# Windowed attention feeding a gated network: the values of a head step in one load of 120 rows of 4 KB, in place of three loads

## The chip, the cores and the metric

The kernel runs on one core of one Trainium2 chip. The metric is the time of one execution on the device in microseconds (us); lower is better.

## The reference: what is computed

Two parts follow each other. The first is attention with B = 4 batches, H = 8 heads, S = 768 positions and D = 64 columns a head, all float32. Each position sees the keys closer than 16 positions and, of every block of 32 positions, one summary: the maximum of the block's keys and the mean of its values (24 summaries a batch).

```python
k_sum = k.reshape(B, H, nb, block, D).max(axis=3)
v_sum = v.reshape(B, H, nb, block, D).mean(axis=3)
scores_l = where(|i - j| < window, scale * q @ k^T, -1e9)
scores_s = scale * q @ k_sum^T + log(block)
a = softmax over concat([scores_l, scores_s])      # with 1e-9 added to the sum
x = a @ concat([v, v_sum])                         # 3072 tokens x 512 columns
h = (x @ w1) * (x @ w2) @ w3                       # 1024 columns
return h @ w_out                                   # 3072 x 512
```

## The kernel before

**Staging.** The kernel works on 6 units of 512 tokens, each with 4 pairs of heads: 24 attention steps `s = (u, p)`. A step covers 4 blocks of 128 tokens. Each block of 128 is worked as two halves `g` of 64 rows; a half needs 96 local keys or values and the 24 summaries, 120 (`KR`) in all. `CUT` is 96 and `NB` is 24.

A step goes through these stages:

- `load_scores` brings `q` and `k`, and `load_values` (line 276) the values `v`, all by DMAs issued on SyncE (SP). `v` has 120 rows (the contraction of the output product), then half, block, and 128 columns: 4 KB a row, in two buffers. For `g = 0` the rows 0 to 95 are local and 96 to 119 summaries; for `g = 1` the rows 0 to 31 are local, 32 to 55 summaries (the gap), 56 to 119 local.
- `load_sums` (line 285) writes the summaries of the values into `v`: for batch 0 two copies on GpSimd (POOL, line 294), for later batches DMAs from SBUF to SBUF on SP (line 291). `gather` (line 306, POOL) writes those of the keys into `k`.
- `scores` (line 319, TensorE, which the profile calls PE), `reduce` (line 333, VectorE, called DVE: mask and minimum), `expose` (line 347, ScalarE, called ACT: the exponentials), `invert` (line 352 on POOL, line 353 on DVE), `normalize_alone` (line 362 on ACT, 364 on DVE) in steps 0 to 7 or `normalize` (line 356, POOL) later.
- `transposes` (line 373, PE, tiles `tp`), `evacuate` (line 378 on ACT for `pt[0]`; line 380 on ACT or 382 on DVE for `pt[1]`, as `SECOND` says), `outputs` (line 393, PE, tile `po`, reads `pt` and `v`), `keep_x` (line 404 on ACT, line 109 on DVE: `x` as a high part and a rounding rest).

**The network.** Every weight arrives as 64-bit words in pieces of 512 KB (`wraw`, line 147) and is rebuilt in `convert`: line 167 on ACT, lines 175 and 178 on DVE, then the high part by a cast on ACT (line 188) and the low part on DVE (line 109, in `low`). `w3 @ w_out` is folded once into `wp` (`fold_weights`; the product leaves PSUM by line 211 on ACT and line 109 on DVE). After the folds, `gate` does the two products of a unit with `w1` and `w2`, and `project` the product with `wp`. All these products are at line 113, three passes each.

**The order.** In the first phase (steps 0 to 7, some 130 us) the order of SP and PE is written by hand: the tables `LOADS` and `WORK` and the tuple `FIRST` say at which count of weight pieces something is loaded, prepared or begun. The order of ACT, DVE and POOL there is chosen when the program is built, by a scheduler that works from its own estimates. In the later loop (steps 8 to 23, by twos) PE, ACT and DVE are in the order of the code. On SP, a DMA takes one of 8 completion semaphores in turn (`DMAHW0` to `DMAHW7` below), and an instruction that waits keeps everything behind it on its engine waiting.

The values of steps 0 to 7 are called for by `LOADS` (15, 21, 25, 28) and `WORK` (29, 37, 42, 46), the summaries by `WORK` alone:

```python
19: [lambda: fetch_sums(0)],
21: [..., lambda: fetch_sums(1)],
22: [..., lambda: fetch_sums(2)],
28: [lambda: fetch_sums(3)],
29: [lambda: fetch_values(4), lambda: fetch_sums(4)],
37: [..., lambda: fetch_values(5), ..., lambda: fetch_sums(5)],
```

Of the kernel before, what the change touches and what calls it, by code (L numbers as in the profile page):

```python
# [19 lines left out]
P = 128  # L20
# [4 lines left out]
CUT = 96  # L25
BIG = -8.0e9
TOKENS = 512
# [43 lines left out]
def attention_moe(ctx, tc, qG, kW, kT, vP, vW, vB, mask, w1, w2, w3T, wo, out):  # L71
    nc = tc.nc
    B, NPAIR, _, S = kT.shape
    NB = S // BLOCK
# [6 lines left out]
    D = P // 2  # L81
    KR = CUT + NB
# [193 lines left out]
    def load_values(u, p):  # L276


        v = sb.tile([KR, 2, NBLK, P], F32, name="v", bufs=2)
        nc.sync.dma_start(v[:CUT, 0], vW[u, p, 0])  # L280
        nc.sync.dma_start(v[: CUT - 64, 1], vW[u, p, 1, : CUT - 64])
        nc.sync.dma_start(v[KR - 64 :, 1], vW[u, p, 1, CUT - 64 :])
        return v

    def load_sums(u, p, v):
# [229 lines left out]
    def fetch_values(s):  # L515
        if s < NS:
            values[s] = load_values(*place(s))
# [257 lines left out]
```

## Time and profile before

| what | value |
|---|---|
| median of 3 runs | 540.87 us (540.83 to 541.28) |
| the profiled execution | 540.83 us, of which the profile's span is 539.0 us |
| mean granted clock of TensorE | 0.989 |
| busy share of the span: PE, weight loads of PE, DVE, ACT, POOL | 96%, 78%, 44%, 44%, 10% |
| DMA of the whole execution | 67.21 MB, mean 125 GB/s |

A row of the profile that gives an instruction has its start in us from the span's beginning, its duration in us, the engine, the line, the operation and the tiles `out<-in`; in brackets stand the idle time of the engine just before it and what ended it. A row `A <- B: x, n, y` counts the waits of A for B: sum in us, how many, and the longest. A row that starts with `a:b` is a window, with the busy time of each engine in it, the granted clock of TensorE (1.00 is full), the DMA share and GB/s.

### The profile page before, as it was taken

The page shows a single profiled execution, that of the slowest core. Times are in us where ns is not written, and L with a number is a line of the kernel's source. Part 1 is how long each engine was busy: PE and PEld are TensorE (multiplying, and loading weights), DVE is VectorE, ACT ScalarE, POOL GpSimd, SP SyncE. Part 2 cuts the span into 40 slices and gives each one's busy share as a digit, 9 for nine tenths or more (in the row PEclk, how much of TensorE's full clock was granted, in tenths as well). Part 3 has the DMA queues.
Part 4 walks back from the last instruction along what each step waited for, and adds up shares of the span by engine and source line. Part 5 has one row for each costly group of instructions (what it writes and reads, how often), then busy time and mean ns, then how long its engine had stood idle before and what let it go on. Part 6 is the DMA issues. An engine that isn't in the chain of part 4 may idle for free.

```text
span 539.0 us, 9912 instructions
## 1 busy us (share of the span) xinstructions
PE 517.9 (96%) x3852; PEld 421.8 (78%) x3852; DVE 237.5 (44%) x686; ACT 238.9 (44%) x688; POOL 56.3 (10%) x103
## 2 busy tenths in 40 slices
PE   2897999999999999999999999999999999999997
PEld 1655777888788888888888888888888888888885
DVE  5868889999503226724244033252042351122210
ACT  5547898887345225226235144253162261222210
POOL 1001221111001101103003002011021020000000
PEclk9988899999999999999999999999999999999999
DMA  8999689956524005544032141050160020000001
GB/s 309 403 348 350 189 270 369 280 183 197 167 96 154 0 1 169 162 128 135 0 111 60 40 152 58 0 157 33 40 190 1 1 75 39 21 21 0 1 19 58
DMA packets 30574, 67.21 MB, mean 125 GB/s; under 512 B 4032, under 2 KB 7616, under 8 KB 30528
## 3 DMA queue, kind: packets, MB, share of 16 engines
q1 hardware_dynamic: 27072, 60.30, 35.2%
q10 hardware_dynamic: 3456, 6.29, 3.1%
q8 instruction: 30, 0.49, 0.4%
q14 instruction: 16, 0.13, 0.1%
HBM read 58.51 MB, written 6.29 MB: 120 GB/s over the span
## 4 chain that ended last, share of the span: by engine, by line
PE 91%; DVE 3%; ACT 3%; DMA 1%; issue 1%; POOL 0%; SPq 0%; POOLq 0%; ACTq 0%
PE mm L113 79%; PE po L393 5%; PE sc L319 4%; PE tp L373 2%; DVE w L109 1%; DMA wraw<-in_w3T_dram 1%; DVE wf L178 1%; ACT w L188 1%; PE means L260 1%; ACT sm L347 1%; DVE wf L175 1%; ACT wf L167 0%; ACT wp L211 0%; DVE wp L109 0%; POOL k L306 0%
## 5 line engine op out<-in xcount | busy, mean ns | idle before, releaser
L113 PE MATMUL mm<-x,w 128*128 128x512 f32 x1152 | 264.9, 390 | 0.0
L113 PEld LDWEIGHTS mm<-x,w 128*128 128x128 f32 x1152 | 215.4, 188 | 45.6 <-issue 0.5
L113 PE MATMUL mm<-wp,h 128*128 128x512 f32 x576 | 133.9, 391 | 0.0
L113 PEld LDWEIGHTS mm<-wp,h 128*128 128x128 f32 x576 | 107.5, 188 | 22.7 <-issue 0.2
L347 ACT ACTIVATE sm<-sm,mx 128x120 f32<-128x120 f32 x192 | 73.6, 387 | 19.9 <-DVE mx L333 19.9
L438 DVE TENSOR_TENSOR g<-mm,g 128x512 f32<-128x512 f32 x48 | 33.1, 689 | 90.6 <-PE mm L113 88.7
L439 ACT CAST h<-g 128x512 fp32r<-128x512 f32 x48 | 29.6, 618 | 87.7 <-DVE g L438 87.7
L113 PE MATMUL mm<-w,w 128*128 128x512 f32 x192 | 54.1, 435 | 12.6 <-ACT w L188 11.5
L113 PEld LDWEIGHTS mm<-w,w 128*128 128x128 f32 x192 | 38.2, 206 | 25.6 <-ACT w L188 13.3
L457 ACT COPY o<-mm 128x512 f32<-128x512 f32 x24 | 14.1, 585 | 81.3 <-PE mm L113 81.3
L109 DVE TENSOR_TENSOR h<-g,h 128x512 fp32r<-128x512 f32 x48 | 35.7, 743 | 24.2 <-ACT h L439 24.0
L435 ACT COPY g<-mm 128x512 f32<-128x512 f32 x48 | 28.0, 584 | 35.6 <-PE mm L113 35.2
L333 DVE CUSTOM_DVE_ANT_0 sm<-sc,mask_sb 128x120 f32<-128x120 f32 x192 | 41.0, 275 | 5.5 <-PE sc L319 5.5
L382 DVE COPY pt<-tp 120x512 f32<-120x512 f32 x19 | 12.4, 686 | 67.7 <-PE tp L373 67.7
L306 POOL COPY k<-ks 128x96 f32<-128x96 f32 (+1 forms) x32 | 10.1, 327 | 252.3 <-DMA k<-in_kW_dram 210.0
L347 ACT ACTIVATION_READ_ACCUMULATOR sm<-sm,mx 128x1 f32 x192 | 36.5, 190 | 0.0
L109 DVE TENSOR_TENSOR x<-po,x 128x512 fp32r<-128x512 f32 x24 | 16.6, 690 | 42.2 <-ACT x L404 42.2
L356 POOL TENSOR_TENSOR sm<-sm,mx 128x960 f32<-128x960 f32 x16 | 29.1, 1820 | 6.0 <-DVE mx L353 5.0
L167 ACT ACTIVATE wf<-wraw 128x512 f32<-128x512 f32 x40 | 26.1, 669 | 6.2 <-DMA wraw<-in_wo_dram 2.7
L188 ACT CAST w<-wf 128x1024 fp32r<-128x1024 f32 (+1 forms) x25 | 21.9, 875 | 12.8 <-DVE wf L178 12.7
L393 PEld LDWEIGHTS po<-pt,v 120*64 120x64 f32 x768 | 23.8, 138 | 4.7 <-issue 2.9
L109 DVE TENSOR_TENSOR w<-wf,w 128x1024 fp32r<-128x1024 f32 (+1 forms) x25 | 25.4, 1014 | 4.4 <-ACT w L188 4.1
(33 smaller groups left out, 281.1 us busy)
## 6 DMA issues: line engine op xcount, KB each, us to landing
k<-in_kW_dram SPq DMA_DIRECT2D x24, 368.0 KB
wraw<-in_w3T_dram SPq DMA_DIRECT2D x16, 512.0 KB
wraw<-in_w_dram SPq DMA_DIRECT2D x16, 512.0 KB
q<-in_qG_dram SPq DMA_DIRECT2D x24, 256.0 KB
raw<-in_kT_dram SPq DMA_DIRECT2D x16, 384.0 KB
out_dram<-o ACTq DMA_DIRECT2D x24, 256.0 KB
v<-in_vW_dram SPq DMA_DIRECT2D x24, 192.0 KB
raw<-in_vB_dram SPq DMA_DIRECT2D x12, 384.0 KB
```

The source lines that it names most:

```text
L109: eng.tensor_tensor(dst, src, hi.bitcast(F32), ALU.subtract)
L113: nc.tensor.matmul(acc, lhsT=a, rhs=b, start=first and i == 0, stop=last and i == len(terms) - 1)
L167: nc.scalar.activation(f[:, k * PIECE : (k + 1) * PIECE], words[:, :, 1].bitcast(F32), AF.Prelu, scale=2.0**-112, alpha=-(2.0**32),)
L188: nc.scalar.copy(hi, f)
L319: nc.tensor.matmul(sc[h][64 * g : 64 * g + 64, i * KR : (i + 1) * KR], lhsT=q[rows, i * P + 64 * g : i * P + 64 * g + 64], rhs=k[rows, i, ...
L333: nc.vector.tensor_tensor_reduce(out=sm[:, j], in0=sc[h][:, i * KR : (i + 1) * KR], in1=mask_sb[:, 0 if blk == 0 else 2 if blk == BLOCKS - ...
L347: nc.scalar.activation(sm[:, j], sm[:, j], AF.Exp, bias=mx[:, 0, j : j + 1], scale=-1.0, accum_out=mx[:, 1, j : j + 1])
L356: nc.gpsimd.tensor_tensor(sm, sm, mx[:, 2].unsqueeze(2).broadcast_to([P, NI, KR]), ALU.mult)
L393: nc.tensor.matmul(po[cols, at : at + 64], lhsT=v[:, g, i, cols], rhs=pt[g][:, (h * NBLK + i) * 64 : (h * NBLK + i + 1) * 64], start=True, ...
L435: nc.scalar.copy(g, a[:, :U])
L438: nc.vector.tensor_tensor(g, acc[1][:, :U], g, ALU.mult)
L439: nc.scalar.copy(h[:, 0], g)
```

## The change

The host lays the values out as they lie on the chip, with zeros in the rows that belong to summaries, and one DMA of 120 rows of 4 KB loads them all. It writes the rows of the summaries too, so the instructions of `load_sums` are ordered behind it. Nothing else is edited. Lines behind the edit have numbers lower by 2.

```diff
@@ load_values
         v = sb.tile([KR, 2, NBLK, P], F32, name="v", bufs=2)
-        nc.sync.dma_start(v[:CUT, 0], vW[u, p, 0])
-        nc.sync.dma_start(v[: CUT - 64, 1], vW[u, p, 1, : CUT - 64])
-        nc.sync.dma_start(v[KR - 64 :, 1], vW[u, p, 1, CUT - 64 :])
+        nc.sync.dma_start(v, vW[u, p])
         return v
@@ on the host
-    wins = wins.reshape(B * S // TOKENS, TOKENS // P, 2, CUT, H // 2, 2 * D)
-    vW = wins.transpose(0, 4, 2, 3, 1, 5)
+    wins = wins.reshape(B * S // TOKENS, TOKENS // P, 2, CUT, H // 2, 2 * D).transpose(0, 4, 3, 2, 1, 5)
+    vW = np.zeros((*wins.shape[:2], CUT + NB, *wins.shape[3:]), v.dtype)
+    vW[:, :, :CUT, 0] = wins[:, :, :, 0]
+    vW[:, :, : CUT - 64, 1] = wins[:, :, : CUT - 64, 1]
+    vW[:, :, CUT + NB - 64 :, 1] = wins[:, :, CUT - 64 :, 1]
```

The order of PE's instructions stays as it was, and SP has 190 rows where it had 240. In the first phase the scheduler puts ACT, DVE and POOL in another order. The numbers behind names of tiles count instructions and shift with the change: `w_895` before is `w_887` after, and `w_977` is `w_969`.

On ACT, around the output product of step 3 (`w_895` and then `w_977` are weights being rebuilt, `wp_87` the last of the 8 folded tiles, `pt` the transposed softmax of step 3), before:

```order
L188 CAST w_895<-wf 128x1024
L167 ACTIVATE wf<-wraw 128x512 x2
L211 CAST wp_87<-mm 128x512
L188 CAST w_977<-wf 128x1024
L378 COPY pt<-tp 120x512
L167 ACTIVATE wf<-wraw 128x512
```

and after:

```order
L188 CAST w_887<-wf 128x1024
L167 ACTIVATE wf<-wraw 128x512 x2
L188 CAST w_969<-wf 128x1024
L211 CAST wp_87<-mm 128x512
L376 COPY pt<-tp 120x512
L167 ACTIVATE wf<-wraw 128x512 x2
```

The cast of the later weight piece has moved ahead of the folded product; the copy `pt` follows both, as before.

On DVE at the same place, before:

```order
L109 TENSOR_TENSOR w_895<-wf,w_895 128x1024
L175 TENSOR_SCALAR wf<-wf 128x1024
L178 SCALAR_TENSOR_TENSOR wf<-wraw,wf 128x512 x2
L109 TENSOR_TENSOR wp_87<-mm,wp_87 128x512
L382 COPY pt<-tp 120x512
L109 TENSOR_TENSOR w_977<-wf,w_977 128x1024
```

and after:

```order
L109 TENSOR_TENSOR w_887<-wf,w_887 128x1024
L175 TENSOR_SCALAR wf<-wf 128x1024
L178 SCALAR_TENSOR_TENSOR wf<-wraw,wf 128x512 x2
L109 TENSOR_TENSOR w_969<-wf,w_969 128x1024
L109 TENSOR_TENSOR wp_87<-mm,wp_87 128x512
L380 COPY pt<-tp 120x512
```

The low part of the later weight piece has moved from behind the copy `pt` to a place ahead of the folded product's low part.

On SP at step 4, with what each instruction waits for (names with `DMAHW` are landings of earlier DMAs by their semaphores, `_49` only part of the name; each load waits for the one that had its semaphore before), before:

```order
L147 DMA wraw<-in_w_dram 128x1024 [waits DMAHW2_49,Activation_49]
L280 DMA v<-in_vW_dram 96x512 [waits DMAHW3_49]
L281 DMA v<-in_vW_dram 32x512 [waits DMAHW4_49]
L282 DMA v<-in_vW_dram 64x512 [waits DMAHW5_49]
L291 DMA v<-vs 24x2x128 [waits DMAHW6_49,DVE_49]
L291 DMA v<-vs 24x2x128 [waits DMAHW7_49]
L147 DMA wraw<-in_w_dram 128x1024 [waits DMAHW0_49,Activation_49]
```

and after:

```order
L147 DMA wraw<-in_w_dram 128x1024 [waits DMAHW2_49,Activation_49]
L280 DMA v<-in_vW_dram 120x1024 [waits DMAHW3_49]
L289 DMA v<-vs 24x2x128 [waits DMAHW4_49,DMAHW3_49,DVE_49]
L289 DMA v<-vs 24x2x128 [waits DMAHW5_49]
L147 DMA wraw<-in_w_dram 128x1024 [waits DMAHW6_49,Activation_49]
```

Two instructions are gone, and the first summary now waits for the load just ahead of it (`DMAHW3_49`), in addition to what it waited for.

## The prediction

> **What bounds the kernel now.** I read the page first (busy shares, the slices, the chain that ended last), then the waits of TensorE, then the order of time around each of them, and last the windows with the granted clock.
>
> ```profile
> PE 517.9 (96%) x3852; PEld 421.8 (78%) x3852; DVE 237.5 (44%) x686; ACT 238.9 (44%) x688; POOL 56.3 (10%) x103
> PE 91%; DVE 3%; ACT 3%; DMA 1%; issue 1%; POOL 0%; SPq 0%; POOLq 0%; ACTq 0%
> ...
> 60.00:90.00 30.00, 29.09 (x330) 22.81 (x327) 26.24 (x78) 26.84 (x83) 6.77 (x13) 1.00 0.83 263
> 90.00:120.00 30.00, 30.00 (x200) 24.30 (x198) 28.19 (x58) 26.29 (x71) 4.35 (x9) 1.00 0.80 249
> ```
>
> The first row is busy time of each engine, the second the shares of the chain. TensorE (PE) is busy 96% of the span. The last two rows are windows (length; busy PE, PEld, DVE, ACT, POOL; granted clock; DMA share; GB/s): from 90 us on PE never stops, so whatever delay or gain reaches it before 90 us stays to the end, one for one. But from 60 to 120 us ScalarE (ACT) and VectorE (DVE) are 88 to 94% busy too. There the kernel has almost no slack in the order in which these two serve PE.
>
> ```profile
> PE mm L113 <- ACT w L188: 11.5, 3, 9.5
> PE tp L373 <- DVE wp L109: 3.9, 2, 2.4
> PE mm L113 <- DVE w L109: 1.1, 2, 0.5
> PE po L393 <- ACT pt L378: 0.7, 2, 0.5
> PE sc L319 <- POOL k L306: 0.4, 1, 0.4
> ```
>
> These are all waits of PE. The first and third are the start, up to 28 us; the first value load is issued only at 25.9 us (rows below), so they cannot change. No wait names a DMA: the transfers that the change touches are not in PE's way. What is left to gain is 3.9 + 0.5 + 0.4 us, what there is to lose is the slack of ACT and DVE.
>
> **The change, part by part.**
>
> *Three loads become one.* 24 times, two DMA instructions of SP go away.
>
> ```profile
> L280 SPq DMA_DIRECT2D v<-in_vW_dram x24: 319/370/892, 25.9 to 434.1; - x24
> L282 SPq DMA_DIRECT2D v<-in_vW_dram x24: 515/598/1173, 26.9 to 435.1; - x24
> 30.00:60.00 30.00, 26.12 (x182) 18.56 (x180) 23.96 (x62) 20.07 (x55) 3.76 (x8) 0.84 1.00 325
> 14.00:30.00 16.00, 12.98 (x49) 9.15 (x49) 13.29 (x21) 8.63 (x15) 0.00 (x0) 0.98 1.03 402
> ACT wf L167 <- DMA wraw<-in_w_dram: 1.4, 1, 1.4
> 118.93 0.69 ACT L167 ACTIVATE wf<-wraw 128x512 f32<-128x512 f32 x1 [1.45 <-DMA wraw<-in_w_dram]
> ```
>
> SP saves the second and third issue, 0.4 to 0.6 us each, some 1.0 us per step, and it is only a queue: that costs nothing and gains nothing unless a transfer is waited for. The bytes grow from 384 to 480 KB. At the 325 GB/s of the window of 30 to 60 us that is 1.51 us for 1.21, at 402 GB/s (the window in which rows of 4 KB prevail) 1.22: between 0 and +0.3 us of DMA time per load. I take 0.1, since the new rows are of the 4 KB kind. The Trainium skill ("DMA: Bandwidth & Descriptors", "Why a DMA increments its semaphore by 16 and not by 1", on how many engines) has a rule against the change: the engines used are the largest number up to 16 that divides the rows, so 120 rows go over 15 engines where 96, 32 and 64 went over 16. By it 8 rows fall to an engine, as in a load of 128 rows, and the sum stays what it is, since no row of PE waits for these loads. The cover is the lead of the loads: the last two rows are the only wait of ACT for a DMA between 30 and 130 us, 1.4 us at 118.93, and PE does not feel it. So 0, bounds 0 to +0.3 for the few loads before 90 us.
>
> *The gap is written twice, so a summary waits for its load.* The single load covers the gap; the copies of summaries on POOL (line 294) and their DMAs on SP (line 291) must wait for it to land, where before they went ahead of it. On POOL the scale of the softmax sums (line 352) and the copies into `k` (line 306) queue behind; on SP the loads that follow. This also leads to another order on POOL.
>
> ```profile
> 60.20 1.26 POOL L294 COPY v<-vs 24x512 f32<-24x512 f32 x2 [1.99 <-PE po L393]
> 61.53 1.36 POOL L306 COPY k<-ks 128x96 f32<-128x96 f32 x2
> 62.73 1.05 PE L319 MATMUL sc<-k,q 64*64 64x120 f32 x32 [0.40 <-POOL k L306]
> 70.24 1.15 PE L393 MATMUL po<-pt,v 120*64 120x64 f32 x32
> ```
>
> Before, the copy of summaries (1.26 us) stood ahead of the keys' copies and PE lost 0.40 us at 62.73. In the new order the keys go first, so this wait goes: -0.40. What is late next is the output product of step 1 (70.24 us): ACT now does one unpacking and one weight cast (0.57 + 0.94) between the exponentials and the copies of the transposes, which then end about 70.4. The 0.40 us is given back there; the sum of both is 0 (-0.4 to +0.4).
>
> *ACT and DVE are put in another order (the term that decides).* The order of the instructions, listed above for both kernels, shows it: the cast of `w_969` stands ahead of `wp_87` and of the copy `pt` on ACT, and its low part ahead of `wp_87` and `pt` on DVE. Before, it went like this:
>
> ```profile
> 81.75 1.05 ACT L188 CAST w<-wf 128x1024 fp32r<-128x1024 f32 x1
> 82.83 1.23 DVE L109 TENSOR_TENSOR w<-wf,w 128x1024 fp32r<-128x1024 f32 x1
> 84.69 1.29 DVE L178 SCALAR_TENSOR_TENSOR wf<-wraw,wf 128x512 uint32<-128x512 uint32 x2
> 85.74 0.59 ACT L211 CAST wp<-mm 128x512 fp32r<-128x512 f32 x1 [1.80 <-PE mm L113]
> 86.22 1.05 ACT L188 CAST w<-wf 128x1024 fp32r<-128x1024 f32 x1
> ...
> 86.36 0.69 DVE L109 TENSOR_TENSOR wp<-mm,wp 128x512 fp32r<-128x512 f32 x1 [0.37 <-ACT wp L211]
> 86.97 0.68 DVE L382 COPY pt<-tp 120x512 f32<-120x512 f32 x1
> 87.17 0.59 ACT L378 COPY pt<-tp 120x512 f32<-120x512 f32 x1
> 87.81 1.15 PE L393 MATMUL po<-pt,v 120*64 120x64 f32 x32 [0.52 <-ACT pt L378]
> 88.89 3.94 PE L113 MATMUL mm<-x,w 128*128 128x512 f32 x16
> ...
> 65.20:83.90 18.70, 18.70 (x188) 14.68 (x187) 16.54 (x43) 18.70 (x63) 3.43 (x8) 1.00 0.81 239
> ```
>
> I put the new order through with these durations. From the exponentials of step 2 to the cast at 81.75, ACT is without a pause before (last row, a window as above: ACT busy 18.70 of 18.70 us) and, I take it, after; the new order has one unpacking more in that stretch (0.57) and one less ahead of it, of which some 0.3 is won (the rest goes to a wait for PE), so it is 0.25 us late: DVE's unpacking of this weight (84.69 + 1.29) ends at 86.23. Only then can the cast start, since it needs it: 86.25 + 1.05 = 87.30. `wp_87` and the first `pt` follow on ACT (0.48 from start to start, then 0.59): the first `pt` is there at 88.3. On DVE the low part starts at 87.33, `wp_87` 1.13 later (the spacing of such rows), `pt` 0.61 after that, and it takes 0.68: the second `pt` is there at 89.75. Of the output product's 16 matmuls two need the first `pt` alone, and the third the second, so 14/16 of 1.08 us follow on 89.8: the gate products start at 90.75 where they started at 88.89. That is +1.86 us on PE, with bounds +0.9 (DVE 0.25 early and its neighbours closer) to +2.4 (ACT late by a whole unpacking). Nothing hides it: PE has no other work in its fixed order.
>
> *The clock.* A stall of PE has a second price here.
>
> ```profile
> 26.00:29.40 3.40, 1.72 (x6) 1.15 (x7) 2.25 (x4) 1.62 (x2) 0.00 (x0) 0.99 1.03 399
> 29.40:32.70 3.30, 3.30 (x9) 2.52 (x9) 2.61 (x6) 1.28 (x3) 0.57 (x1) 0.50 1.06 357
> 46.40:49.80 3.40, 0.99 (x5) 0.40 (x3) 3.00 (x6) 3.40 (x9) 0.24 (x1) 1.00 1.08 241
> 49.80:53.20 3.40, 1.94 (x36) 1.81 (x39) 3.37 (x6) 1.80 (x4) 0.00 (x0) 0.50 1.02 355
> ...
> 28.41 5.53 PE L113 MATMUL mm<-w,w 128*128 128x512 f32 x16 [0.53 <-DVE w L109]
> 88.89 13.92 PE L113 MATMUL mm<-x,w 128*128 128x512 f32 x60
> ```
>
> The columns are as above; the granted clock is the third from the right. Both times that PE was busy for only 0.99 or 1.72 of 3.40 us, the next 3.4 us were granted half the clock. Sixteen products took 5.53 us across such a stretch, where 60 take 13.92, so 16 take 3.7: one stretch costs 1.84 us. In the new order PE idles from 87.3 (87.81 less 0.52) to 88.3 and from 88.4 to 89.8, 2.3 us within 3.4, which is between the two cases that brought the clock down: +1.84 us (0 if the stretches are cut so that neither holds enough of it). By the Trainium skill ("TensorE: Matmul & The Clock Gate", "Why this matters for your kernels") only gaps over some 3 us between bursts bring the clock down; the gap of 1.43 us and the one of 0.53 before 28.41 speak against that. By it the term would be 0.
>
> **Sum.** 540.83 (the profiled execution: span 539.0 and 1.8 around it; the median of the runs shown is 540.87, the same) + 0 (loads) + 0 (POOL) + 1.86 (output product of step 3) + 1.84 (clock) = 544.5 us.
>
> **The rivals.**
>
> A. The stall comes without the clock's share: 540.83 + 1.86 = 542.7. For it: the idle time could fall across two stretches, or the half clock after 49.8 us could be released one stretch earlier, since DVE's work around PE's stops there is in another order too (-1.84 on the forecast, which gives the same time). This is also what the skill's rule of 3 us gives. Against it: both short gaps of the trace were followed by half clock.
>
> B. No stall (the other side): PE's 24 fold products of step 3 end at 85.7 as before, and if DVE has unpacked `w_969` by 84.7 the cast is done before `wp_87` can start. Then `pt` is early, the 0.52 at 87.81 goes as well, and the time is 540.83 - 0.52 = 540.3 or, with the clock released earlier at 53 us, 538.5. It decides if ACT reaches the cast at 81.75 by 80.5, 1.3 us sooner. Against it: ACT has no pause in that window from which to take 1.3 us.
>
> C. SP stands still. Summaries of steps 4 and 5 are DMAs and now wait on SP until the load before them lands.
>
> ```profile
> 89.50 0.42 SPq L280 DMA_DIRECT2D v<-in_vW_dram  x1
> 91.72 0.98 SPq L291 DMA_DIRECT2D v<-vs  x1
> 114.74 0.42 SPq L280 DMA_DIRECT2D v<-in_vW_dram  x1
> 125.44 1.15 PE L393 MATMUL po<-pt,v 120*64 120x64 f32 x32
> ```
>
> Before, the summaries were issued 2.2 us after their load at 89.50. The weight load just ahead of the one at 114.74 let ACT go at 118.93, some 4.6 us after its issue. A summary of step 5 would then be issued at 114.74 + 4.6 = 119.3 at the earliest, the second one about 1 us later, and land some 4.6 us after that: at 124.9, for a product at 125.44. The cover is 0.5 us, and 3.7 more where PE is late anyway: 4.2 over two landings. It is gone if a landing takes over 6.7 us. Two more loads of 512 KB ahead (1.3 us each at 402 GB/s) at both landings add 5.2 us, 1.0 beyond the cover: 545.5.
>
> **How the numbers follow.** My forecast (stall and clock) 0.43, A 0.24, B 0.19, C on top of the stall 0.14. From B at 540.3 to 538.5 I leave most out (0.19 less what lies near A); the range reaches from a stall at its lower bound, +0.9 without the clock (541.7, less 0.4 for the POOL term: 541.3), to C with a stall at its upper bound (545.5 + 0.5 = 546.0). 0.2% is 1.08 us, about what a measurement of this kernel can tell from no change. Faster by that: B with the clock, 0.07. Within: the rest of B, 0.12. Slower: 0.81.
>
> **What would show it.** In the new profile: PE's output product of step 3 (near 88 us) waits over 1 us for DVE's `pt` (line 380 there), and the ACT cast of `w` before it waits for DVE; the wait of 0.40 for POOL is gone; a window of 3.4 us after it has the clock at 0.50, with PE's mean clock near 0.98; from there PE is again without a pause. The rows of the value load show 24 instructions and no engine waiting for them. I am wrong if PE's wait there stays under 0.6 us, if the ACT row of the cast comes before the product of folds ends, or if a new wait of PE names a DMA.

## The result and the profile after

The changed kernel takes 552.43 us (median of 4 runs, 551.14 to 554.62), the kernel before 540.85 in the same comparison: ratio 1.0234, 95% interval 1.0211 to 1.0258. Forecast were 544.5 us and 541.3 to 546.0, so the sign was right and the size was not. The profiled execution has a span of 550.8 us, 11.8 more than before. Single disturbed executions (866 to 1042 us) of the kernel before and of two kernels below are left out of all medians, and for these two kernels no profile is read.

The shares of the chain from the page of the changed kernel, and windows of it as in the prediction:

```profile
PE 77%; DMA 9%; DVE 7%; ACT 5%; issue 1%; SPq 1%; POOL 0%; DVEq 0%; POOLq 0%; ACTq 0%
60.00:90.00 30.00, 25.69 (x286) 19.67 (x284) 24.45 (x64) 25.43 (x77) 5.39 (x10) 0.98 0.93 271
120.00:150.00 30.00, 25.83 (x173) 20.18 (x172) 20.60 (x46) 14.60 (x40) 4.18 (x10) 0.94 0.62 185
```

PE's share of the chain fell from 91 to 77%, and DMA's rose from 1 to 9%: transfers now stand on the way to PE, though PE's waits before named none. From 60 to 90 us PE works 25.69 of 30 us (29.09 before), and from 120 to 150 us, where it had no pause at all, 25.83.

The waits of PE in the changed kernel:

```profile
PE mm L113 <- DVE g L436: 4.2, 2, 3.6
...
PE mm L113 <- DVE h L109: 0.5, 1, 0.5
```

The wait of 0.4 for POOL is gone, as forecast. The output product of step 3 now waits 2.95 + 1.20 us (rows below), and the gate products wait 4.2 us for DVE's `g`, a wait that was not in the list before (nor was that for `h`).

Where the 11.8 us came in is seen from the start of the same instruction of PE in both traces (PE's order is unchanged). Before:

```profile
86.24 0.95 PE L319 MATMUL sc<-k,q 64*64 64x120 f32 x28
102.74 0.68 PE L373 MATMUL tp<-ident,sm 64*120 64x64 f32 x16
142.44 0.68 PE L373 MATMUL tp<-ident,sm 64*120 64x64 f32 x16
236.75 1.16 PE L373 MATMUL tp<-ident,sm 64*120 64x64 f32 x32
```

After, with the rows of the stops between them:

```profile
84.60 1.05 PE L317 MATMUL sc<-k,q 64*64 64x120 f32 x32
88.60 0.34 PE L391 MATMUL po<-pt,v 120*64 120x64 f32 x4 [2.95 <-issue]
90.13 1.76 PE L391 MATMUL po<-pt,v 120*64 120x64 f32 x28 [1.20 <-DVE pt L380]
91.82 3.78 PE L113 MATMUL mm<-x,w 128*128 128x512 f32 x8
107.48 0.68 PE L371 MATMUL tp<-ident,sm 64*120 64x64 f32 x16
131.08 1.15 PE L391 MATMUL po<-pt,v 120*64 120x64 f32 x32
140.09 10.04 PE L113 MATMUL mm<-x,w 128*128 128x512 f32 x36 [3.56 <-DVE g L436]
153.46 0.68 PE L371 MATMUL tp<-ident,sm 64*120 64x64 f32 x16
248.55 1.16 PE L371 MATMUL tp<-ident,sm 64*120 64x64 f32 x32
```

| place | lag of PE behind the kernel before, us | added there |
|---|---|---|
| scores of step 4 (84.60 against 86.24) | -1.64 | -1.64 |
| transposes of step 4 (107.48 against 102.74), behind the output product of step 3 | +4.74 | +6.38 |
| output product of step 5 (131.08 against 125.44) | +5.64 | +0.90 |
| transposes of step 6 (153.46 against 142.44), behind the stop of 3.56 us | +11.02 | +5.38 |
| transposes of the pair 10 and 11 (248.55 against 236.75) | +11.80 | +0.78 |

### The profile page after: what moved, and what is told of

Read it like the earlier page. It is cut to its first block, busy times and chain, and to the rows that moved or that the text cites. A ratio compares the mean times of both kernels' runs of the same rounds, so it can differ in the third digit from the quotient of the medians.

```text
span 550.8 us, 9843 instructions
## 1 busy us (share of the span) xinstructions
PE 521.2 (95%) x3852; PEld 423.2 (77%) x3852; DVE 237.5 (43%) x686; ACT 239.4 (43%) x688; POOL 57.4 (10%) x103
## 3 DMA queue, kind: packets, MB, share of 16 engines
q1 hardware_dynamic: 24552, 62.65, 36.5%
## 4 chain that ended last, share of the span: by engine, by line
PE 77%; DMA 9%; DVE 7%; ACT 5%; issue 1%; SPq 1%; POOL 0%; DVEq 0%; POOLq 0%; ACTq 0%
PE mm L113 67%; PE po L391 4%; PE sc L317 3%; DMA v<-in_vW_dram 3%; DVE w L109 2%; PE tp L371 2%; ACT sm L345 2%; DMA raw<-in_vB_dram 2%; DMA wraw<-in_w_dram 2%; DVE wf L178 1%; ACT w L188 1%; DMA wraw<-in_w3T_dram 1%; DMA k<-in_kW_dram 1%; PE means L260 1%; DVE vs L247 1%
## 5 line engine op out<-in xcount | busy, mean ns | idle before, releaser
L113 PE MATMUL mm<-x,w 128*128 128x512 f32 x1152 | 268.8, 394 | 4.2 <-DVE g L436 4.2
L113 PEld LDWEIGHTS mm<-x,w 128*128 128x128 f32 x1152 | 217.8, 190 | 51.3 <-ACT sm L360 4.0
L113 PE MATMUL mm<-w,w 128*128 128x512 f32 x192 | 52.8, 427 | 12.9 <-ACT w L188 11.9
L391 PE MATMUL po<-pt,v 120*64 120x64 f32 x768 | 27.2, 228 | 4.6 <-issue 3.0
```

Source lines behind the costliest of these rows:

```text
L113: nc.tensor.matmul(acc, lhsT=a, rhs=b, start=first and i == 0, stop=last and i == len(terms) - 1)
L391: nc.tensor.matmul(po[cols, at : at + 64], lhsT=v[:, g, i, cols], rhs=pt[g][:, (h * NBLK + i) * 64 : (h * NBLK + i + 1) * 64], start=True, ...
```

## The experiments

In the kernels whose order was held, line numbers are 9 higher than in the kernel with the same loads, so lines 178, 306, 352 and 393 of the kernel before are 187, 315, 361 and 402 with three loads and 187, 313, 359 and 400 with one. All were compared with the kernel before on the same chip (539.2 to 539.8 us there); "old order" means that of the kernel before, "new order" that of the changed kernel. Only the orders named were held. Where one load, or three that cover the gap, ran with the old order of ACT and DVE in steps 0 to 7, POOL was in an order of the scheduler's own, which has another instruction than the kernel before at 28 to 30 of POOL's 103 places; no run has such loads with all three old orders. An order was held by edges of issue order between neighbours of one engine; the table has the places of the instructions:

```diff
+def pin(tc):
+    for name, order in PINNED.items():
+        mine = [i for i in tc.nc.cur_bb.bb.instructions if i.engine == getattr(mybir.EngineType, name)]
+        order = [mine[int(k)] for k in order.split()]
+        for a, b in zip(order, order[1:]):
+            ...
+            tc.add_manual_dep(b, a.name, info, reason="order")
```

**Order and loads apart.** Three loads with the new order of ACT, DVE and POOL; one load with the old order of ACT and DVE.

> Three loads as before, but ACT, DVE and POOL held in the order that the kernel with one load has. If the order of ACT and DVE is what stops PE at step 3's output product, that stop (3.0 + 1.2 us after the change) and the half clock behind it (1.8 us) are here too, and nothing more: 543.5 to 545.5 us, with no wait of PE over 1 us for DVE behind 100 us. If the new load itself or SP's waits cause all of it, the time is that of before, 540.9.

Measured: 551.56 us, ratio 1.0230 (1.0207 to 1.0254), 6 us above the upper end of the expectation. The order alone, with every load as it was, costs as much as the whole change. Its timeline shows a stop that the expectation had left out:

```profile
136.40 0.26 POOL L315 COPY k<-ks 128x96 f32<-128x96 f32 x1 [9.01 <-DMA k<-in_kW_dram]
136.75 0.23 POOL L361 TENSOR_SCALAR mx<-mx 128x8 f32<-128x8 f32 x1
139.26 10.59 PE L122 MATMUL mm<-x,w 128*128 128x512 f32 x36 [5.76 <-DVE g L447]
```

The new order of POOL puts the copy of the keys of step 8 ahead of the scale of step 6's softmax sums. The copy waits for a load; the scale, the reciprocal on DVE and everything behind it on DVE wait with it, and PE stops for 5.76 us. In the kernel before, the scale ran first:

```profile
127.60 0.23 POOL L352 TENSOR_SCALAR mx<-mx 128x8 f32<-128x8 f32 x1 [4.35 <-ACT sm L347]
133.48 0.26 POOL L306 COPY k<-ks 128x96 f32<-128x96 f32 x1 [4.74 <-DMA k<-in_kW_dram]
```

> One load as after the change, but ACT and DVE held in the order of the kernel with three loads; POOL's order is left to the scheduler. If SP standing still behind the summaries is the second cause, the three late stops of PE stay (0.9 + 5.4 + 0.8 us after the change): 547 to 548.5, and PE's wait at step 3 is under 0.6 us. If the order of ACT and DVE is the only cause, 540.9.

Measured: 545.81 us, ratio 1.0123 (1.0092 to 1.0155), below the expectation for a second cause (547 to 548.5) and above that for the order alone (540.9). PE waits 2.81 us at step 3, where under 0.6 was expected, so the wait there does not need the new order of ACT and DVE. (The profiled execution took 550.04 us, the longest of six; its rows show more loss than the median has.)

```profile
88.28 1.58 POOL L301 COPY v<-vs 24x512 f32<-24x512 f32 x2 [5.58 <-DMA v<-in_vW_dram]
90.39 1.16 PE L400 MATMUL po<-pt,v 120*64 120x64 f32 x32 [2.81 <-ACT pt L385]
```

The summaries on POOL wait for the load till 88.28, the cast on ACT waits 1.79 us for DVE, and PE for the copy behind it.

**POOL's order taken out.** Three loads, ACT and DVE in the new order, POOL in the old:

> Three loads; ACT and DVE in the order of the changed kernel, POOL in the order of the kernel before. With POOL in the new order too, the time was 551.6 us, with a stop of PE of 5.8 us near 139 us. If that stop comes from POOL's order alone (the softmax scale of step 6 behind the copy of keys of step 8, which waits for a load), it goes here with its half clock, 7 to 8 us, and the stop at step 3 stays: 541.5 to 544. If the order of ACT and DVE makes both, 551.5.

Measured: 545.94 us, ratio 1.0126 (1.0106 to 1.0147), 2 us above the upper end. So POOL's order is worth 5.6 us of the 12.3 of the whole new order (551.56 - 545.94), a little less than the 7 to 8 expected, and ACT's and DVE's the rest:

```profile
86.43 0.34 PE L402 MATMUL po<-pt,v 120*64 120x64 f32 x4 [1.52 <-ACT pt L387]
87.91 1.76 PE L402 MATMUL po<-pt,v 120*64 120x64 f32 x28 [1.15 <-DVE pt L391]
88.00:91.00 3.00, 3.00 (x31) 2.65 (x32) 2.38 (x13) 1.28 (x6) 0.23 (x1) 0.50 0.97 342
```

This is the stop at step 3 of the forecast, without the load: `pt` late by the cast ahead of it, and half clock behind it (last row, a window as above). From the scores of step 4 to its transposes PE falls behind by 3.75 us here, and by 3.57 with POOL's new order too. Later PE still waits 1.73 us for DVE `g`, near 139 us.

**POOL's order mended in the changed kernel.** The same one instruction is moved there:

```diff
 POOL:  scale of step 5; copies v (step 5); copies k (step 7);
+       scale of step 6;
        copies v (step 6); copy k (step 8);
-       scale of step 6; ...
```

> The changed kernel with its order of ACT and DVE; in POOL's order one instruction is moved, the softmax scale of step 6, ahead of the value summaries of step 6 and the keys of step 8, behind which it stands. If POOL's order makes the late stop (3.6 us and its half clock of 1.8), the time is 552.4 - 5.4 = 547 us (546 to 548). If SP's waits make it, since the loads themselves are late, 551 to 553.

Measured: 552.67 us, ratio 1.0256 (1.0225 to 1.0287): nothing is gained. With one load the place has a second cause (the profiled execution, 556.66 us, is again the longest of six):

```profile
137.97 0.23 POOL L359 TENSOR_SCALAR mx<-mx 128x8 f32<-128x8 f32 x1 [3.90 <-ACT sm L354]
144.40 0.95 DVE L239 TENSOR_REDUCE ks<-raw 128x24 f32<-128x768 f32 x1 [3.11 <-DMA raw<-in_kT_dram]
...
149.16 4.59 PE L122 MATMUL mm<-x,w 128*128 128x512 f32 x12 [2.60 <-DVE g L445]
```

The scale now waits only for ACT. But DVE's key summaries wait 3.11 us, and further on 1.60 us, for loads that SP issued late, DVE's `g` stands behind them, and PE stops there instead.

**SP's waits taken out.** Other DMAs stand between a load and its summaries:

```diff
-        29: [lambda: fetch_values(4), lambda: fetch_sums(4)],
-        31: [lambda: load_second(7)],
+        29: [lambda: fetch_values(4)],
+        31: [lambda: load_second(7), lambda: fetch_sums(4)],
+        33: [lambda: fetch_values(5)],
-        37: [..., lambda: fetch_values(5), lambda: fetch(7), ...],
+        37: [..., lambda: fetch(7), ...],
         ... likewise for steps 6 and 7
```

> One load, the order of ACT and DVE as after the change, but in steps 4 to 7 other DMAs stand between a value load and its summaries (the loads of steps 5 to 7 are called for 4, 4 and 3 counts sooner, the summaries of step 4 two counts later). If SP's waits at the summaries cause the loss behind 95 us, 7.1 us of it go: 545 to 546, and PE's wait of 3.6 us for DVE g goes. If the load as such is slow (its landing), at most 1 to 2 us go: 550 to 552.

Measured: 548.60 us, ratio 1.0173 (1.0150 to 1.0196). The waits for DVE `g` are gone, but only 3.3 us of the 7.1 (1.0234 to 1.0173), which lies between the two expectations: PE now waits 1.25 us for DVE `h` at 229 us, and step 3 keeps its stop (2.11 + 1.20 us).

> Both: the summaries behind other DMAs as in the run above, and ACT and DVE in the order of the kernel with three loads. If order and SP's waits are the two causes and nothing else is, the time is that of before or a little less, 539.5 to 541.5. If the 120 rows or the 96 KB more per load cost by themselves, 543 or more.

Measured: 543.20 us, ratio 1.0065 (1.0042 to 1.0088), above the range given for two causes and nothing else and in that for a cost of the rows or bytes themselves. Against the same load with its summaries where they were (1.0123) SP's waits are worth 3.1 us here. What is left is one stop at step 3:

```profile
83.49 0.67 ACT L176 ACTIVATE wf<-wraw 128x512 f32<-128x512 f32 x1 [1.53 <-DMA wraw<-in_w_dram]
87.95 1.16 PE L400 MATMUL po<-pt,v 120*64 120x64 f32 x32 [2.29 <-ACT pt L385]
```

A weight piece arrives 1.53 us late for ACT. That points to the load, which is moved beside it, but no run shows it alone. PE also came to this place 1.63 us sooner than before (scores of step 4 at 84.61 against 86.24), so the product starts only 0.14 later (87.95 against 87.81); most of the 1.74 us by which the next transposes are late is the half clock behind the stop.

**The 120 rows.** The same load with 128 rows, eight of zeros, once with the old order and once as the only edit to the changed kernel, where the scheduler keeps the new order:

```diff
-        v = sb.tile([KR, 2, NBLK, P], F32, name="v", bufs=2)
+        v = sb.tile([P, 2, NBLK, P], F32, name="v", bufs=2)
         nc.sync.dma_start(v, vW[u, p])
-        return v
+        return v[:KR]
```

> One load as in the run with the old order of ACT and DVE (545.8 us), but of 128 rows of 4 KB, eight of them never read. In the kernels with 120 rows a packet of 4 KB of a value load takes some 262 ns, worked out from the sums by size, where the others take 193. If the 120 rows cause that (they divide by 15, not by 16), the packets of 4 KB come down to about 195 ns on average from 215, the weight piece ahead of step 3 lands some 2 us sooner, and the time is 542 to 543.5. If it is only the number of bytes, it is 546 or more.

Measured: 543.46 us, ratio 1.0074 (1.0047 to 1.0101), 2.4 us less than with 120 rows in this order, as expected if the rows count and not the bytes; the two intervals just overlap, so the next run decides.

> The changed kernel with 128 rows in place of 120 (eight rows of zeros that nothing reads), and nothing else: ACT, DVE and POOL keep the order of the changed kernel. If the order is the larger cause, the time stays near that of three loads in this order, 550 to 552 us. If the slow landing over 120 rows is the larger one, 546 to 547, with the late waits of PE for DVE g gone.

Measured: 547.54 us, ratio 1.0149 (1.0125 to 1.0172), between the two expectations: 8 rows of zeros more bring the ratio from 1.0234 to 1.0149, 4.6 us. The queue rows of the pages of the changed kernel and of the one with 128 rows and the old order (packets, MB, share of 16 engines' span):

```profile
q1 hardware_dynamic: 24552, 62.65, 36.5%
```

```profile
q1 hardware_dynamic: 24768, 63.44, 34.0%
117.72 0.38 SPq L289 DMA_DIRECT2D v<-in_vW_dram  x1
123.58 1.67 SPq L298 DMA_DIRECT2D v<-vs  x2
```

And that of the kernel before:

```profile
q1 hardware_dynamic: 27072, 60.30, 35.2%
```

With the spans (550.8, 542.3, 539.0 us) the engines worked 201.0, 184.4 and 189.7 us on this queue. Put down to the 24 loads, one load of 120 rows costs 0.47 us more than the three it replaces ((201.0 - 189.7) / 24), one of 128 rows 0.22 us less, though it moves 32 KB more than that of 120. The load of step 5 landed within 5.9 us (123.58 - 117.72), where SP could go on with the summaries; with 120 rows, in the changed kernel, within 7.25 (128.30 - 121.05, rows further below). By the landings that the traces record, the median of the 24 loads is 7.7 us from issue with 120 rows, 6.5 with 128 and 4.7 for the last of the three loads before.

**Both mended, and step 3.** 128 rows, old order, summaries behind other DMAs; then also the values of step 3 loaded one weight piece sooner (`28: fetch_values(3)` becomes `27`):

> 128 rows, the old order of ACT and DVE, and the summaries of steps 4 to 7 behind other DMAs. The run with 128 rows alone had one stop of PE left, 3.6 us at step 3 with 1.5 us of half clock behind it, and none from SP's waits. If SP's waits no longer matter there, nothing is gained: 542.5 to 544. If they still did, 540 to 541.

Measured: 544.05 us, ratio 1.0086 (1.0061 to 1.0111); its interval overlaps that of 128 rows alone, so with 128 rows SP's waits cost nothing that can be seen. What stops PE at step 3 here:

```profile
82.95 2.71 POOL L301 COPY v<-vs 24x512 f32<-24x512 f32 x2 [3.46 <-DMA v<-in_vW_dram]
84.21 2.00 DVE L187 SCALAR_TENSOR_TENSOR wf<-wraw,wf 128x512 uint32<-128x512 uint32 x2
87.87 1.37 PE L400 MATMUL po<-pt,v 120*64 120x64 f32 x32 [2.78 <-issue]
```

POOL's copies of the summaries, which must now wait for the load, run beside DVE's work on a weight (the low part, line 184, then the unpacking), and both copies and unpacking are slow: 2.71 us (1.26 for the same copies at 60.20 before) and 2.00 us (1.29).

> As the run with 128 rows and later summaries (544.05 us), but the values of step 3 are loaded one weight piece sooner. There POOL's copies of the summaries of step 3 wait for that load, run from 82.95 us on and take 2.71 us where the same two copies took 1.25 in the kernel before, and DVE's unpacking beside them takes 2.00 where it took 1.29; the cast on ACT waits 2.1 us for it and PE 2.8. If that collision is what is left at step 3, the copies end ahead of the unpacking, PE's wait falls to 1.5 to 2 and the time to 541 to 543 us. If the landing of the weight piece or the bytes are, it stays at 543.5 to 545.

Measured: 544.45 us, ratio 1.0093 (1.0076 to 1.0109): the second expectation. The collision is gone (the unpacking takes 1.29 us again), and the loss is where it was:

```profile
82.97 1.22 DVE L256 TENSOR_REDUCE vs<-raw 96x32 f32<-96x1024 f32 x1 [1.36 <-DMA raw<-in_vB_dram]
89.56 1.98 PE L400 MATMUL po<-pt,v 120*64 120x64 f32 x32 [3.05 <-ACT pt L385]
```

The value load went ahead of the blocks for the means of the next batch, and now DVE waits 1.36 us for those, ahead of the same unpacking.

**The wait without the one load.** Three loads that cover the gap, old order; then with the summaries behind other DMAs:

```diff
-        nc.sync.dma_start(v, vW[u, p])
+        nc.sync.dma_start(v[:, 0], vW[u, p, :, 0])
+        nc.sync.dma_start(v[: CUT - 64, 1], vW[u, p, : CUT - 64, 1])
+        nc.sync.dma_start(v[CUT - 64 :, 1], vW[u, p, CUT - 64 :, 1])
```

> Three loads of 2 KB rows that cover the gap too (120, 32 and 88 rows in place of 96, 32 and 64), so the summaries wait for them as they do for the one load; ACT and DVE in the old order. If the wait of the summaries costs by itself, the loss of the one load in this order stays, 544 to 546 us. If it costs only because the one load of 120 rows lands late, 539.5 to 541.

Measured: 545.35 us, ratio 1.0114 (1.0089 to 1.0139): in total as much as the one load in this order (1.0123), but not in the same places:

```profile
87.32 1.36 PE L402 MATMUL po<-pt,v 120*64 120x64 f32 x32 [1.36 <-issue]
225.76 15.07 PE L122 MATMUL mm<-wp,h 128*128 128x512 f32 x65 [1.38 <-DVE h L118]
```

The stop at step 3 is half as long (1.36 us against 2.81) and brings no half clock, and of the 4 us that this profile has lost by the pair 10 and 11 some 3.5 come behind the transposes of step 6. Nor does the run vary the gap alone: two of its loads have 120 and 88 rows, and rows of such counts are themselves a suspect by the runs with 128 rows. So it shows that three loads with long cover can cost as much, not that the gap is what costs.

> Three loads that cover the gap (545.35 us), and the summaries of steps 4 to 7 behind other DMAs. If SP standing at the summaries makes the loss of that kernel, it goes: 540 to 541.5 us, the rest being step 3, whose summaries are POOL's. If the bytes of the gap make it, 544 to 546.

Measured: 544.85 us, ratio 1.0097 (1.0066 to 1.0127): no clear change, though steps 4 to 7 lose nothing more. It fits the expectation for the bytes, but the place does not: most of the loss in this profile lies in the loop behind step 7, which was not edited:

```profile
220.18 2.34 DVE L256 TENSOR_REDUCE vs<-raw 96x32 f32<-96x1024 f32 x2 [3.25 <-DMA v<-vs]
225.71 15.03 PE L122 MATMUL mm<-wp,h 128*128 128x512 f32 x65 [1.38 <-DVE h L118]
```

The summaries read `vs`. Delayed behind their load, they hold the tile, DVE waits 3.25 us before it may write the next one, and `h` behind it is late for PE.

**The first phase and the loop apart.** One load only from step 8 on, or only up to step 7:

```diff
+        if u < 2:      # the other kernel: u >= 2
+            nc.sync.dma_start(v[:CUT, 0], vW[u, p, :CUT, 0])
+            ... and the other two loads
+        else:
             nc.sync.dma_start(v, vW[u, p])
```

> Three loads in steps 0 to 7, one load of 120 rows in steps 8 to 23; ACT and DVE keep the order of the kernel before. If the loss is made in the first phase, where ACT, DVE and the DMA queues are full, only the wait of PE for DVE h near 230 us can come (0.8 to 1.7 us in the runs with one load): 539.3 to 541 us. If a landing over 120 rows or a standing SP costs wherever it is, 543 or more.

Measured: 541.28 us, ratio 1.0033 (1.0016 to 1.0049). PE's only new wait in its profile is 0.31 us, for `h` at 222 us; the rest of the 1.8 us is not seen there.

> The other half: one load in steps 0 to 7, three loads from step 8 on; ACT and DVE keep the order of the changed kernel. If the first phase makes the loss, 550.5 to 552.5 us.

Measured: 553.04 us, ratio 1.0247 (1.0219 to 1.0274): one load in steps 0 to 7 is enough for the whole loss.

**A version meant to beat both.** Three loads; ACT and DVE in the new order up to the scores of step 4, in the old behind them, and the copy `pt` of step 3 ahead of the cast on ACT:

> Three loads and POOL as before; ACT and DVE in the new order up to the scores of step 4, in the old one behind them, and at step 3 ACT takes the last folded product and the copy of the transposes ahead of the cast of the next weight. The new order brought PE 1.1 to 1.6 us sooner to the scores of step 4, and the 0.5 us in front of step 3's output product goes: 537.5 to 538.5 us if nothing takes it back, 539 to 540 if the clock is halved somewhere else.

Measured: 540.19 us, ratio 1.0021 (1.0004 to 1.0037), which is no gain; without a profile it stays open what took back the expected 1 to 2 us. No version with one load came under the kernel before.

## Why the prediction was wrong, and where it was right

The step that failed is the two terms of the sum that were put at 0, "+ 0 (loads) + 0 (POOL)", and with them the claim that from step 3 on PE is again without a pause. The sum put 3.7 us at step 3 and nothing behind it; measured are 4.74 us up to the transposes of step 4 and 7.06 behind them. In place of the zeros the runs show POOL's order at 5.6 us, SP's waits at 3.1 to 3.3 and 120 rows in place of 128 at 4.6, amounts that overlap.

Of the signs named in advance, the waits at step 3, the half clock and the end of POOL's 0.40 us came. Not so the rest: POOL waited 7.65 us for the load of step 3 (row below) and SP 7.25 for that of step 5, and PE had further stops.

- **The order of ACT and DVE at step 3: right in mechanism, the near time in part luck.** Forecast were the first `pt` at 88.3, the second at 89.75 and the gate products at 90.75. In the changed kernel:

```profile
84.74 1.71 DVE L178 SCALAR_TENSOR_TENSOR wf<-wraw,wf 128x512 uint32<-128x512 uint32 x2
85.04 1.89 POOL L292 COPY v<-vs 24x512 f32<-24x512 f32 x2 [7.65 <-DMA v<-in_vW_dram]
86.49 1.04 ACT L188 CAST w<-wf 128x1024 fp32r<-128x1024 f32 x1 [2.89 <-DVE wf L178]
87.91 0.59 ACT L376 COPY pt<-tp 120x512 f32<-120x512 f32 x1
89.31 0.68 DVE L380 COPY pt<-tp 120x512 f32<-120x512 f32 x1
89.00:92.40 3.40, 2.27 (x29) 2.11 (x30) 2.85 (x13) 1.10 (x3) 0.22 (x1) 0.50 1.04 407
92.40:95.80 3.40, 3.40 (x9) 2.65 (x8) 3.25 (x10) 2.39 (x13) 1.17 (x2) 0.50 0.95 269
```

The copies end at 88.50 and 89.99, and the gate products start at 91.82. The cast waits for DVE's unpacking, as forecast; the unpacking took 1.71 instead of 1.29 beside POOL's copies, which the sum did not have. Forecast for this place and the clock was a lag of 3.7 us, and 4.74 was measured (second row of the table). That is near because two misses offset: 6.38 us were added here, and PE had come 1.64 sooner, which the sum had as 0. The order alone, with three loads, adds 3.57 to 3.75 us, what the forecast gave it; the rest came with the load. (The 16 matmuls that the prediction counts are 32 in the rows, 4 and then 28; the share of 14/16 is right.)

- **The clock: right, and larger.** Half clock came at once, and for two stretches instead of one (a stretch costs 5.53 - 3.71, 1.82 us and not 1.84, which changes nothing); the first fell on the output product itself (28 matmuls in 1.76 us). In the changed kernel one gap was 2.95 us, but with three loads and the new order of ACT and DVE the clock fell around gaps of 1.52 and 1.15 us too. The Trainium skill's rule to leave no gaps of over some 3 us between bursts ("TensorE: Matmul & The Clock Gate", "Why this matters for your kernels") is therefore too lax for the traces here, and rival A falls with it.
- **POOL's order: the step was worked at one place only.** Near step 1 the wait of 0.40 is gone as forecast, but it was not given back: PE reaches the scores of step 4 1.64 us sooner. And the same list of POOL has the scale of step 6 behind the copy of the keys of step 8, and the prediction did not follow it that far. The two runs with three loads and the new order of ACT and DVE price POOL's order at 5.6 us (551.56 - 545.94). It is the largest thing that could have been read from the orders in advance.
- **The loads "at 0": wrong.** The bound of +0.3 us a load was too low (0.47 measured), and "no row of PE waits for these loads" looked for direct waits. The DMA engines were 0.83 busy from 60 to 90 us before and 0.93 after, and transfers beside or behind the load came later: a weight piece for ACT (1.53 us in one run above), the key blocks for DVE (3.11 in another). That the sum "stays what it is" with 120 rows, 8 to an engine as with 128, was wrong in this too: 128 rows alone gave back 4.6 us.
- **Rival C: right that SP stands still, wrong in where it costs.** The prediction priced only the landing of the summary against the output product that reads it, and gave 1.0 us. In the changed kernel the chain goes another way:

```profile
121.05 0.39 SPq L280 DMA_DIRECT2D v<-in_vW_dram  x1
128.30 1.66 SPq L289 DMA_DIRECT2D v<-vs  x2
131.05 0.41 SPq L299 DMA_DIRECT2D k<-in_kW_dram  x1
137.44 0.26 POOL L304 COPY k<-ks 128x96 f32<-128x96 f32 x1 [1.06 <-DMA k<-in_kW_dram]
137.79 0.23 POOL L350 TENSOR_SCALAR mx<-mx 128x8 f32<-128x8 f32 x1
138.05 0.20 DVE L351 RECIPROCAL mx<-mx 128x8 f32<-128x8 f32 x1 [3.94 <-POOL mx L350]
```

The load lands some 7.2 us after its issue, beyond the 6.7 that the rival named as its condition. SP stands, the keys that are queued behind the summaries are issued at 131.05, POOL's copy waits for them, the scale of step 6 stands behind that copy, DVE behind the scale, and PE behind DVE: 3.56 us and a stretch of half clock, 5.38 in the table. The product that the rival priced (131.08) did not wait at all, since PE was 5.64 us late by then.

- **Rival B** (no stall) is out: the stop came in the changed kernel and in the run that had the new order of ACT and DVE alone.

The causes do not add up: the new order alone costs 12.3 us (551.56 - 539.22), one load in the old order of ACT and DVE 6.6 (545.81 - 539.22), and the change, which has both, no more than the first. Two delays that end at the same instruction are paid once; that fits this, and the run in which moving POOL's scale alone won nothing. Open is how the 3.5 to 5 us that stay with one load in the old order (ratios 1.0065 to 1.0093), in the profiles nearly all at step 3, part into bytes, landing, POOL's wait, POOL's own order, which was never held there, and half clock after PE came early; each edit only changed what was late.

## What to carry to other kernels

A transfer that PE does not wait for can still cost where the DMA engines are nearly full, since others come later; price an added byte or a slow load by what stands behind it. When a load starts to overlap a later write, follow the whole in-order queue of every engine that waits, to the end of the phase and not to the first reader. And where a scheduler orders the engines, compare the order for every engine through all steps that have no slack: here an order that nobody had asked for cost as much as the whole change.

## What the runs showed of the hardware

- A load of 120 rows of 4 KB took more of the DMA engines' time than one of 128 (0.69 us a load, (201.0 - 184.4) / 24) and landed later (a median of 7.7 against 6.5 us). By the Trainium skill ("DMA: Bandwidth & Descriptors", "Why a DMA increments its semaphore by 16 and not by 1") 120 rows go over 15 engines and 128 over 16, 8 rows each either way. The traces fit these counts: the queue has 9 packets more a load with 128 rows ((24768 - 24552) / 24), 8 for the rows and one more, as if each engine closed a load with a packet of its own. But 8 rows each would make no difference of this size. What differs is the time of a packet: some 262 ns for the 4 KB of such a load with 120 rows and 166 with 128, an estimate from the sums by size, in which the other packets of 4 KB are taken to be as long as before (193). Why stays open.
- The clock: the records of it in the traces change in stretches of 3.41 us. In the 15 traces that are read, from 36 us on, all 30 stretches at full clock in which PE was busy for 1.47 us or less were followed by half clock, and none of the 2131 in which it was busy for 1.49 or more; before 36 us the border is less sharp (it fell behind 1.77 and held behind 1.44). So it is not one gap that counts here but the sum of the busy time, and where the stretches are cut: the gap of 1.36 us at step 3 with three loads over the gap brought no half clock.
- POOL's copies of 24 x 512 and DVE's unpacking with two inputs slowed each other: in the changed kernel 1.89 us where such a pair of copies took 1.26, and 1.71 where the unpacking took 1.29. The Trainium skill ("GPSIMD Engine Reference", "1. Specifications") says that POOL shares its interfaces to SBUF with VectorE, with contention where an instruction has two inputs in SBUF; the rows agree.
